# Output stores on ScalarE's queue, first weights kept by quarters, smaller feed-forward blocks and a changed plan in a recurrence-plus-feed-forward kernel

## Chip, cores and metric

One core of a Trainium2 chip. The metric is the device time of one execution in microseconds; a kernel's figure is the median of several executions. Executions of one kernel on one chip spread by about 1% here, some by up to 2%. An execution that lies more than 1.5% above the fastest of the same kernel is called slow, and the ratios leave it out. The granted clock is the share of its full clock that the profile shows for TensorE. Beside each kernel the kernel before was run in the same rounds, because chips differ: the medians of the kernel before lie between 197.7 and 199.8 us. Ratios in this document are the mean time of one kernel's fast runs over that of the other's of the same rounds, so they are not quite the ratio of the medians that are quoted. Brackets hold the 95% interval.

## What is computed

```python
def _attn_ref(r, k, v, w, u):                 # 4 batches, 8 heads, 768 steps, 48 wide
    state = np.zeros((B, H, D, D))
    for t in range(S):
        cur = einsum('bhd,bhe->bhde', u * k_t, v_t)
        y_t = einsum('bhd,bhde->bhe', r_t, state + cur)
        state = w_t[..., None] * state + einsum('bhd,bhe->bhde', k_t, v_t)

def _moe_ref(x, w_in, w_out):                 # x 3072x384, w_in 384x2048, w_out 2048x384
    h = x @ w_in
    g = np.maximum(0.01 * h, h)
    return g @ w_out
```

The recurrence's output, heads side by side, is x. Inputs and output are float32; the kernel multiplies in bfloat16.

## The kernel before

The 3072 tokens go in 24 chunks of 128. Each chunk has some twenty steps (log of the decays, cumulative sums, exponentials, the scaled r and k called `kr`, their transpose `rkT`, scores, mask, y, the new state, and y transposed into `xT`). Feed-forward blocks of 128 or 256 tokens follow: hidden matmuls into PSUM, activations on ScalarE, output matmuls, a copy, a store. (PSUM is where this kernel's matmuls write.)

Nothing is ordered by hand. Every step is entered with its engine, the time it is thought to take, the lag until others may use its result, and a rank; a small simulation (`Order`) sends out, one by one, whichever step can start first, and the kernel is emitted in that order. Each engine, and the one DMA queue of the sync engine, then works strictly in it.

```python
class Order:
    # cut: add, alias, ready
    def run(self, pools):
        # cut
        while any(todo.values()):
            best = None
            for eng, names in todo.items():
                loads = False
                for rank, seq, name in names:
                    # loads keep their order; stores and transposes may pass them
                    if eng == "DMA" and name[0] not in ("store", "rkT", "xT"):
                        if loads:
                            continue
                        loads = True
                    t = ready(name)
                    if t is None:
                        continue
                    t = max(t, free[eng])
                    key = (t, rank, seq)
                    if best is None or key < best[0]:
                        best = (key, eng, (rank, seq, name))
            # cut: send out best, advance free[eng], note the end

    w_in_b = const.tile([128, KT, FF], BF16, name="w_in_b")        # KT = 3, FF = 2048

    def cast_w_in(q):                                              # four quarters, on VectorE
        nc.vector.tensor_copy(out=w_in_b[:, :, q * FQ : (q + 1) * FQ], in_=stage["in", q][:])

    def a_rkT(i):                                                  # chunks 0 to 10
        if i < EARLY:                                              # EARLY = 5
            nc.scalar.copy(out=rkT[:], in_=att[i]["trp"][:])
        else:
            nc.vector.tensor_copy(out=rkT[:], in_=att[i]["trp"][:])

    def a_rkT_dma(i):                                              # chunks 11 to 23
        nc.sync.dma_start_transpose(out=rkT[:]..., in_=kr_b[i % NB3][:]...)

    sizes = [256, 256, 128, 128, 256, 128, 128, 256, 256, 256, 256, 256, 256, 256]

    def m_store(q, ts):
        nc.sync.dma_start(out=out[row : row + 128, :], in_=osbs.pop((q, ts))[:])

    Y_BY_DMA = range(15, NCH)
    WARM = 40.0          # filler matmuls on an idle tile keep TensorE's clock up until here
    RACT = 50            # rank of the feed-forward activations
    # cut
        add((x, n), "DMA", 1.06, load_in, n, x, lag=1.95, needs=past_user)        # w, r, k, v
            step("rkT", "DMA", 1.3, a_rkT_dma, "kr", *past(3, "mix"), lag=3.3)
            step("xT", "DMA", 0.6, a_ytr_dma, "ysb", "vsc", "t2", "st", lag=3.3)
            add(("store", q, ts), "DMA", 0.6, m_store, q, ts, lag=1.9, rank=-1, needs=[("copy", q, ts)])
```

Of the kernel before, what the change touches and what calls it, by code (L numbers as in the profile page):

```python
# [9 lines left out]
BF16 = mybir.dt.bfloat16  # L10
# [5 lines left out]
class Order:  # L16


    def __init__(self):
        self.steps = {}  # L20
        self.names = {}

    def add(self, name, eng, took, f, *args, lag=0.06, rank=0.0, needs=(), takes=()):
        self.steps[name] = (eng, took, f, args, lag, rank, list(needs), takes)
# [11 lines left out]
    def run(self, pools):  # L36
# [33 lines left out]
        while any(todo.values()):  # L70
            best = None
            for eng, names in todo.items():
                loads = False
                for rank, seq, name in names:
                    if eng == "DMA" and name[0] not in ("store", "rkT", "xT"):
                        if loads:
                            continue
                        loads = True
                    t = ready(name)
                    if t is None:  # L80
                        continue
                    t = max(t, free[eng])
                    key = (t, rank, seq)
                    if best is None or key < best[0]:
                        best = (key, eng, (rank, seq, name))
# [15 lines left out]
def kernel(  # L101
# [24 lines left out]
    NIN = 12  # L126
    EARLY = 5

# [3 lines left out]
    gpool = ctx.enter_context(tc.tile_pool(name="gpool", bufs=2))  # L132
    opool = ctx.enter_context(tc.tile_pool(name="opool", bufs=4))
    ps_cum = ctx.enter_context(tc.tile_pool(name="ps_cum", bufs=1, space=bass.MemoryType.PSUM))
# [13 lines left out]
    ukb = const.tile([128, DM], F32, name="ukb")  # L148
    w_in_b = const.tile([128, KT, FF], BF16, name="w_in_b")
    w_out_b = const.tile([128, NFT, NOUT], BF16, name="w_out_b")  # L150
# [37 lines left out]

    NQ = 4
    FQ = FF // NQ  # L190
# [17 lines left out]
    def cast_w_in(q):  # L208
        nc.vector.tensor_copy(out=w_in_b[:, :, q * FQ : (q + 1) * FQ], in_=stage["in", q][:])  # L209

# [176 lines left out]

    sizes = [256, 256, 128, 128, 256, 128, 128, 256, 256, 256, 256, 256, 256, 256]
    assert sum(sizes) == B * S
# [6 lines left out]
    def m_hid(q, j, nj):  # L396
        mb, t0 = sizes[q], starts[q]
        if j == 0:
            gts[q] = gpool.tile([128, NFT, mb], BF16, name="gt", tag="gt")
        hp = hps[q, j] = ps_mlp.tile([128, nj, mb], F32, name="hp", tag="mlp")  # L400
        for jj in range(nj):
            for t in range(KT):
                nc.tensor.matmul(  # L403
                    hp[:, jj, :], lhsT=w_in_b[:, t, (j + jj) * 128 : (j + jj + 1) * 128],
                    rhs=xT[:, t, t0 : t0 + mb], start=(t == 0), stop=(t == KT - 1),
                )
# [17 lines left out]
    def m_store(q, ts):  # L424
        row = starts[q] + ts * 128
        nc.sync.dma_start(out=out[row : row + 128, :], in_=osbs.pop((q, ts))[:])



    BY_DMA = range(11, NCH)  # L430
    Y_BY_DMA = range(15, NCH)
    WARM = 40.0
    RCAST = -1
    RACT = 50
    order = Order()
    add = order.add
    add("const", "POOL", 2.2, constants, rank=-1)
    users = []
    queue = [('in', 0), ('u', 0), ('in', 1), ('in', 2), ('w_in', 0), ('in', 3), ('w_in', 1), ('w_in', 2), ('w_in', 3), ('in', 4), ('w_out', 0), ('w_out', 1), ('w_out', 2), ('w_out', 3)] + [("in", i) for i in range(5, NCH)]
    for kind, n in queue:  # L440
# [4 lines left out]
        if kind == "in":  # L445
            for x in ("w", "r", "k", "v"):
                add((x, n), "DMA", 1.06, load_in, n, x, lag=1.95, needs=past_user)
            users.append(("done", n))
# [5 lines left out]
    for i in range(NCH):  # L454
# [17 lines left out]
        step("exn", "ACT", 0.52, a_exn, "neg", "exp")  # L472
        step("kr", "DVE", 1.05, a_kr, "exp", "exn", "k", "r", *past(3, "trans", "kv"))
        step("t1", "POOL", 1.0, a_t1, "r", ("u",), *past(2, "t2"))
        step("t2", "POOL", 1.15, a_t2, "t1", "k", *past(2, "diag"))
        step("vb", "ACT" if early else "POOL", 0.53, a_vb, "v", *past(3, "mix", "kv"))
        step("diag", "DVE", 0.55, a_diag, "t2", *past(3, "vsc"))
        step("vsc", "POOL", 0.86, a_vsc, "diag", "v", *past(3, "ysb"))
        if i in BY_DMA:
            step("rkT", "DMA", 1.3, a_rkT_dma, "kr", *past(3, "mix"), lag=3.3)  # L480
            order.alias(("trans", i), ("rkT", i))
        else:
            step("trans", "PE", 0.45, a_trans, "kr", *past(1, "rkT"), lag=0.3)
            step("rkT", "ACT" if early else "DVE", 1.0 if early else 0.69, a_rkT, "trans", *past(3, "mix"))
# [14 lines left out]
        if i in Y_BY_DMA:  # L499
            step("xT", "DMA", 0.6, a_ytr_dma, "ysb", "vsc", "t2", "st", lag=3.3)  # L500
            order.alias(("ytr", i), ("xT", i))
# [5 lines left out]
    for q, mb in enumerate(sizes):  # L507
# [8 lines left out]
        for ts in range(mb // L):  # L516
            for part in range(NQ):
# [5 lines left out]
            add(("copy", q, ts), "ACT", 0.48, m_copy, q, ts, rank=0, needs=[("out", q, ts, NQ - 1)]  # L523
                + [("store", *x) for x in tiles[-5:-4]])
            add(("store", q, ts), "DMA", 0.6, m_store, q, ts, lag=1.9, rank=-1, needs=[("copy", q, ts)])
    steps = order.run({"att": 3, "mlp": 3})
# [41 lines left out]
```

## Time and profile before

| | kernel before |
|---|---|
| median of 4 executions | 198.12 us (197.86 to 198.21) |
| profiled span, mean granted clock | 195.5 us, 1.000 |
| first output matmul starts | 43.82 us |
| 65th output matmul starts (4 of 24 output tiles done) | 59.80 us |
| last output copy starts | 192.21 us |
| TensorE time lost after 42 us | 10.9 us |
| of that, gaps over 0.25 us | 5.0 us |

The rows from "first output matmul" on are read from the starts of the single matmuls. They cut the run in two: a **start**, up to the 65th output matmul, and a **later part**, from there to the last copy (132.4 us here). "Lost" is the time to the next matmul's start beyond what the matmul itself takes.

The wait list of the sync engine's queue, kernel before. Its columns are: what waited, for whom, us in total, how many times, the longest. Its totals run over the whole span, so they include waits after the last load, which cost nothing; they are read for their order.

```profile
SPq L426 <- ACT osb L422: 24.4, 14, 7.4
SPq L299 <- DVE kr L256: 10.3, 10, 1.9
```

So two kinds of entries hold up the loads: stores (L426) that wait for their copy, and transposes (L299) that wait for `kr`.

The groups by shape of VectorE, kernel before (count | busy us, mean ns of one | idle before):

```profile
L209 DVE CAST w_in_b<-ws 128x1536 bf16<-128x1536 f32 x4 | 7.0, 1746 | 1.0 <-DMA ws<-in_moe_w_in_dram 1.0
```

And the chain that ended last, summed by engine, with the landing time of stores from the list of DMA issues:

```profile
PE 50%; DMA 20%; DVE 11%; SPq 9%; issue 5%; ACT 4%; DVEq 0%; ACTq 0%
...
out_dram<-osb SPq DMA_DIRECT2D x24, 192.0 KB, 2.2
```

### The profile page before, as it was taken

How to read it: one execution, taken by the hardware profiler on the slowest of the kernel's cores; microseconds unless marked ns; L12 is line 12 of the kernel's file. 1: busy time of each engine (PE TensorE's matmuls, PEld its weight loads, DVE VectorE, ACT ScalarE, POOL GpSimd, SP SyncE). 2: the span in 40 equal slices, each digit the busy share in tenths (PEclk: the TensorE clock that was granted, in tenths of full speed). 3: DMA queues.
4: the chain of work that ended last, by engine and by line, in shares of the span. 5: the costliest groups of instructions: out<-in, count | busy, mean ns of one | idle time of the engine just before them, and what ended most of it. 6: DMA issues, size and time to landing. Idle time of an engine off the chain costs nothing.

```text
span 195.5 us, 4886 instructions
## 1 busy us (share of the span) xinstructions
PE 182.2 (93%) x1921; PEld 130.0 (67%) x1926; DVE 115.7 (59%) x182; ACT 112.7 (58%) x219; POOL 111.3 (57%) x141
## 2 busy tenths in 40 slices
PE   7999697889999989999999997997999999999993
PEld 2455465765777758877777784774775876868661
DVE  2176997546479969996876776728457547300000
ACT  3565645872747476875587792482682762727310
POOL 3399554307457799999579688724757848100000
PEclk9999999999999999999999999999999999999999
DMA  6999899999499999999999998979989996221022
GB/s 126 203 188 249 225 376 149 358 330 142 129 198 210 195 203 215 187 169 190 156 230 207 184 161 167 213 149 168 213 181 190 217 166 126 64 62 40 3 80 80
DMA packets 124647, 34.70 MB, mean 177 GB/s; under 512 B 117840, under 2 KB 123088, under 8 KB 124624
## 3 DMA queue, kind: packets, MB, share of 16 engines
q1 hardware_dynamic: 124624, 34.38, 87.7%
q8 instruction: 15, 0.25, 0.5%
q14 instruction: 8, 0.07, 0.1%
HBM read 25.36 MB, written 4.72 MB: 154 GB/s over the span
## 4 chain that ended last, share of the span: by engine, by line
PE 50%; DMA 20%; DVE 11%; SPq 9%; issue 5%; ACT 4%; DVEq 0%; ACTq 0%
PE hp L403 21%; PE op L415 21%; DMA in<-in_w_dram 10%; DMA in<-in_k_dram 10%; SPq L184 7%; DVE mt L317 5%; DVE kr L256 2%; PE at L309 2%; DVE w_in_b L209 2%; ACT lw L224 1%; PE y L334 1%; PE cum L229 1%; PE trp L288 1%; PE ytr L375 1%; PE kv L347 1%
## 5 line engine op out<-in xcount | busy, mean ns | idle before, releaser
L403 PE MATMUL hp<-xT,w_in_b 128*128 128x256 bf16 (+1 forms) x672 | 71.5, 257 | 2.4 <-ACT gt L409 1.3
L415 PE MATMUL op<-w_out_b,gt 128*128 128x384 bf16 x384 | 68.8, 326 | 0.0
L409 ACT ACTIVATE gt<-hp 128x512 bf16<-128x512 f32 x96 | 55.8, 597 | 14.7 <-PE hp L403 12.6
L403 PEld LDWEIGHTS <-w_in_b 128*128 128x128 bf16 x672 | 56.2, 98 | 11.4 <-DVE w_in_b L209 2.0
L415 PEld LDWEIGHTS <-gt 128*128 128x128 bf16 x384 | 35.5, 98 | 20.6
L256 DVE TENSOR_TENSOR kr<-e,in 128x768 bf16<-128x768 f32 x24 | 28.1, 1169 | 19.5 <-DMA in<-in_k_dram 10.2
L317 DVE TENSOR_TENSOR mt<-at,tri 128x512 bf16<-128x512 f32 x48 | 31.0, 683 | 12.7 <-PE at L309 12.5
L264 POOL TENSOR_TENSOR t<-t,in 128x384 f32<-128x384 f32 x24 | 31.5, 1311 | 8.5 <-DMA in<-in_k_dram 7.4
L260 POOL TENSOR_TENSOR t<-in,ukb 128x384 f32<-128x384 f32 x24 | 24.0, 1000 | 16.6 <-DMA in<-in_r_dram 10.6
L365 POOL TENSOR_TENSOR st<-tt,e 48x192 bf16<-48x192 f32 x40 | 24.0, 600 | 16.6 <-DVE tt L355 15.1
L422 ACT COPY osb<-op 128x384 f32<-128x384 f32 x24 | 11.4, 477 | 30.5 <-PE op L415 30.2
L279 POOL TENSOR_TENSOR vsc<-in,diag 128x384 f32<-128x384 f32 x24 | 22.0, 916 | 8.6 <-DVE diag L275 5.8
L224 ACT ACTIVATE lw<-in 128x384 bf16<-128x384 f32 x24 | 12.5, 523 | 14.1 <-DMA in<-in_w_dram 14.1
L534 PE MATMUL scratch<-idle 128*128 128x512 bf16 x63 | 18.3, 415 | 1.4 <-DVE idle L166 1.3
L342 DVE TENSOR_TENSOR ysb<-y,vsc 128x384 bf16<-128x384 f32 x24 | 13.2, 552 | 5.4 <-PE y L334 4.1
L249 ACT ACTIVATE e<-cum 128x388 f32<-128x388 f32 x24 | 11.9, 496 | 7.4 <-PE cum L231 6.5
L275 DVE TENSOR_REDUCE diag<-t 128x8 f32<-128x384 f32 x24 | 13.1, 544 | 4.8 <-POOL t L264 4.6
L242 DVE SCALAR_TENSOR_TENSOR neg<-cum,lw 128x384 f32<-128x384 f32 x19 | 10.5, 553 | 9.0 <-ACT e L249 8.7
L271 POOL CAST vb<-in 128x384 bf16<-128x384 f32 x19 | 10.3, 542 | 4.2 <-DMA in<-in_v_dram 3.7
L252 ACT ACTIVATE e<-neg 128x384 f32<-128x384 f32 x19 | 9.9, 523 | 3.6 <-DVE neg L242 3.6
L534 PEld LDWEIGHTS <-idle 128*128 128x128 bf16 x68 | 6.5, 103 | 7.4 <-issue 1.9
L334 PE MATMUL y<-vb,mt 128*128 128x48 bf16 x192 | 9.2, 184 | 1.9 <-DVE mt L317 1.7
(43 smaller groups left out, 137.7 us busy)
## 6 DMA issues: line engine op xcount, KB each, us to landing
in<-in_w_dram SPq DMA_DIRECT2D x24, 192.0 KB, 4.3
in<-in_r_dram SPq DMA_DIRECT2D x24, 192.0 KB, 4.4
in<-in_k_dram SPq DMA_DIRECT2D x24, 192.0 KB, 4.3
in<-in_v_dram SPq DMA_DIRECT2D x24, 192.0 KB, 4.3
out_dram<-osb SPq DMA_DIRECT2D x24, 192.0 KB, 2.2
ws<-in_moe_w_in_dram SPq DMA_DIRECT2D x4, 768.0 KB, 6.7
ws<-in_moe_w_out_dram SPq DMA_DIRECT2D x4, 768.0 KB, 7.4
rkT<-kr SPq DMA_TRANSPOSE x13, 3.2
```

Source lines behind the costliest of these rows:

```text
L184: nc.sync.dma_start(out=ins[i][name], in_=src[b, :, c * L : (c + 1) * L, :].rearrange("h p d -> p h d"))
L224: nc.scalar.activation(out=lw_b[i % NB3][:, :, 0:D], in_=ins[i]["w"], func=AF.Ln)
L256: nc.vector.tensor_tensor(out=kr_b[i % NB3][:, :, 0:D], in0=e, in1=ins[i]["kr"], op=ALU.mult)
L260: nc.gpsimd.tensor_tensor(out=t1[:], in0=flat(ins[i]["r"]), in1=ukb[:], op=ALU.mult)
L264: nc.gpsimd.tensor_tensor(out=flat(t2[:]), in0=att[i]["t1"][:], in1=flat(ins[i]["k"]), op=ALU.mult)
L279: nc.gpsimd.tensor_tensor(out=vsc[:], in0=ins[i]["v"], in1=att[i]["diag"][:].unsqueeze(2).to_broadcast([128, H, D]), op=ALU.mult,)
L317: nc.vector.tensor_tensor(out=att[i]["mt"][:, x], in0=att[i]["ats"][x][:], in1=tri[:].unsqueeze(1).to_broadcast([128, NP, 128]), op=ALU.mult,)
L365: nc.gpsimd.tensor_tensor(out=sn[r0 : r0 + D, :, x * D : (x + 1) * D], in0=tt[r0 : r0 + D, :, x * D : (x + 1) * D], in1=el[r0 : r0 + D, :] ...
L403: nc.tensor.matmul(hp[:, jj, :], lhsT=w_in_b[:, t, (j + jj) * 128 : (j + jj + 1) * 128], rhs=xT[:, t, t0 : t0 + mb], start=(t == 0), stop= ...
L409: nc.scalar.activation(out=gts[q][:, j : j + nj, :], in_=hps.pop((q, j))[:], func=AF.Prelu, alpha=0.01)
L415: nc.tensor.matmul(ops[q, ts][:], lhsT=gts[q][:, j, ts * 128 : (ts + 1) * 128], rhs=w_out_b[:, j, :], start=(j == 0), stop=(j == NFT - 1),)
L534: nc.tensor.matmul(scratch[:], lhsT=idle[:, 0:128], rhs=idle[:], start=True, stop=True)
```

## The change

The intent: take stores that wait for a copy out of the queue that feeds the loads, and issue them on ScalarE right behind that copy; make each quarter of the first weights one run, so that its cast is quick; make most feed-forward blocks 128 tokens, so that a late chunk holds up less. With it come small numbers of the plan.

```diff
-    w_in_b = const.tile([128, KT, FF], BF16, name="w_in_b")
+    w_in_b = const.tile([128, NQ, KT, FF // NQ], BF16, name="w_in_b")
-        nc.vector.tensor_copy(out=w_in_b[:, :, q * FQ : (q + 1) * FQ], in_=stage["in", q][:])
+        nc.vector.tensor_copy(out=w_in_b[:, q], in_=stage["in", q][:])

-    sizes = [256, 256, 128, 128, 256, 128, 128, 256, 256, 256, 256, 256, 256, 256]
+    sizes = [256, 256, 128, 128, 128, 128, 128, 128, 128, 128, 128, 128, 128, 128, 128, 256, 128, 256, 256]

-        nc.sync.dma_start(out=out[row : row + 128, :], in_=osbs.pop((q, ts))[:])
+        nc.scalar.dma_start(out=out[row : row + 128, :], in_=osbs.pop((q, ts))[:])
# cut: the store becomes an "issue" step of ScalarE; output buffers 4 -> 6

# the plan's numbers
+                    if eng == "DMA" and waits and loads:      # waits: store, rkT or xT
+                        t += self.slack[name[0]]              # 1.2 us for rkT and xT
-            step("rkT", "DMA", 1.3, a_rkT_dma, "kr", *past(3, "mix"), lag=3.3)
+            step("rkT", "DMA", 1.6, a_rkT_dma, "kr", *past(3, "mix"), lag=2.2)
-            step("xT", "DMA", 0.6, a_ytr_dma, "ysb", "vsc", "t2", "st", lag=3.3)
+            step("xT", "DMA", 0.6, a_ytr_dma, "ysb", "vsc", "t2", "st", lag=2.4)
-    EARLY = 5
+    EARLY = 4
-    WARM = 40.0
+    WARM = 18.0
-    RACT = 50
+    RACT = 12
-    Y_BY_DMA = range(15, NCH)
+    Y_BY_DMA = range(14, NCH)
# cut: three planned times, 1.06 -> 1.07, 1.05 -> 1.08, 1.15 -> 1.2
```

The slack says: when a load could go now, plan a transpose 1.2 us after the time at which its data are thought to be ready.

More of the change, by code (lines that the diff above doesn't have):

```diff
@@ L21, in __init__ @@
         self.names = {}
+        self.slack = {}
     def add(self, name, eng, took, f, *args, lag=0.06, rank=0.0, needs=(), takes=()):
@@ L74, in run @@
                 for rank, seq, name in names:
-                    if eng == "DMA" and name[0] not in ("store", "rkT", "xT"):
+                    waits = name[0] in ("store", "rkT", "xT")
+                    if eng == "DMA" and not waits:
                         if loads:
@@ L126 @@
     NIN = 12
-    EARLY = 5
+    NOUTB = 6
+    NQ = 4
+    EARLY = 4
     const = ctx.enter_context(tc.tile_pool(name="const", bufs=1))
@@ L132 @@
     gpool = ctx.enter_context(tc.tile_pool(name="gpool", bufs=2))
-    opool = ctx.enter_context(tc.tile_pool(name="opool", bufs=4))
+    opool = ctx.enter_context(tc.tile_pool(name="opool", bufs=NOUTB))
     ps_cum = ctx.enter_context(tc.tile_pool(name="ps_cum", bufs=1, space=bass.MemoryType.PSUM))
@@ L187, in load_u @@
         nc.sync.dma_start(out=ukb[:], in_=u.rearrange("h d -> (h d)").partition_broadcast(128))
-    NQ = 4
     FQ = FF // NQ
@@ L401, in m_hid @@
         for jj in range(nj):
+            wq, f0 = divmod((j + jj) * 128, FQ)
             for t in range(KT):
                 nc.tensor.matmul(
-                    hp[:, jj, :], lhsT=w_in_b[:, t, (j + jj) * 128 : (j + jj + 1) * 128],
+                    hp[:, jj, :], lhsT=w_in_b[:, wq, t, f0 : f0 + 128],
                     rhs=xT[:, t, t0 : t0 + mb], start=(t == 0), stop=(t == KT - 1),
@@ L425, in m_store, with m_stored @@
         row = starts[q] + ts * 128
-        nc.sync.dma_start(out=out[row : row + 128, :], in_=osbs.pop((q, ts))[:])
+        nc.scalar.dma_start(out=out[row : row + 128, :], in_=osbs.pop((q, ts))[:])
+    def m_stored(q, ts):
+        pass
     BY_DMA = range(11, NCH)
-    Y_BY_DMA = range(15, NCH)
-    WARM = 40.0
+    Y_BY_DMA = range(14, NCH)
+    WARM = 18.0
     RCAST = -1
-    RACT = 50
+    SLACK = 1.2
+    RACT = 12
     order = Order()
+    order.slack = {"rkT": SLACK, "xT": SLACK, "store": 0.0}
     add = order.add
     add("const", "POOL", 2.2, constants, rank=-1)
+    users = []
+    users = []
     users = []
@@ L446 @@
             for x in ("w", "r", "k", "v"):
-                add((x, n), "DMA", 1.06, load_in, n, x, lag=1.95, needs=past_user)
+                add((x, n), "DMA", 1.07, load_in, n, x, lag=1.95, needs=past_user)
             users.append(("done", n))
@@ L472 @@
         step("exn", "ACT", 0.52, a_exn, "neg", "exp")
-        step("kr", "DVE", 1.05, a_kr, "exp", "exn", "k", "r", *past(3, "trans", "kv"))
+        step("kr", "DVE", 1.08, a_kr, "exp", "exn", "k", "r", *past(3, "trans", "kv"))
         step("t1", "POOL", 1.0, a_t1, "r", ("u",), *past(2, "t2"))
-        step("t2", "POOL", 1.15, a_t2, "t1", "k", *past(2, "diag"))
+        step("t2", "POOL", 1.2, a_t2, "t1", "k", *past(2, "diag"))
         step("vb", "ACT" if early else "POOL", 0.53, a_vb, "v", *past(3, "mix", "kv"))
@@ L523 @@
             add(("copy", q, ts), "ACT", 0.48, m_copy, q, ts, rank=0, needs=[("out", q, ts, NQ - 1)]
-                + [("store", *x) for x in tiles[-5:-4]])
-            add(("store", q, ts), "DMA", 0.6, m_store, q, ts, lag=1.9, rank=-1, needs=[("copy", q, ts)])
+                + [("store", *x) for x in tiles[-NOUTB - 1 : -NOUTB]])
+            add(("issue", q, ts), "ACT", 0.3, m_store, q, ts, rank=-1, needs=[("copy", q, ts)])
+            add(("store", q, ts), "DMA", 0.6, m_stored, q, ts, lag=1.9, rank=-1, needs=[("issue", q, ts)])
     steps = order.run({"att": 3, "mlp": 3})
```

## The prediction

> **What bounds the kernel now.** I read the page first (busy shares, slices), then the groups by shape, the chain that ended last, the sync engine's queue in order of time, and the starts of the single matmuls.
>
> ```profile
> PE 182.2 (93%) x1921; PEld 130.0 (67%) x1926; DVE 115.7 (59%) x182; ACT 112.7 (58%) x219; POOL 111.3 (57%) x141
> ...
> PE   7999697889999989999999997997999999999993
> ...
> PEclk9999999999999999999999999999999999999999
> DMA  6999899999499999999999998979989996221022
> ```
>
> TensorE is busy nearly throughout at full clock; the DMA engines are full until slice 34 (about 163 us) and then nearly idle. So there are two candidates, matmuls and input loads. "Busy" does not decide it, because matmuls overlap. The chain gives their real rate:
>
> ```profile
> 91.44 1.34 PE hp L403 x24
> ...
> 98.76 1.32 PE hp L403 x12
> ...
> 171.28 5.20 PE op L415 x32
> ```
>
> A 128-token hidden matmul takes 1.34/24 = 56 ns, a 256-token one 1.32/12 = 110 ns, an output one (384 columns) 5.20/32 = 163 ns. I gave every matmul in the trace its columns/2.4 ns + 2.5 ns and called the rest of the time to the next start "lost". Lost time: 7.7 us before 33 us (and 13.2 us of filler matmuls on the idle tile there), 2.2 us from 33 to 42, and from 42 us to the last matmul at 192.2 only 11.0 us out of 150. So from 42 us on the kernel is **matmul-bound with small leaks**; before that it is bound by what must happen ahead of the matmuls. Of the 11.0 us, 5.0 us are seven gaps over 0.25 us: at 68.4 (0.93), 75.4 (0.31), 119.6 (1.19), 134.2 (1.10), 135.3 (0.57), 149.6 (0.58) and 163.8 us (0.31). All but the one at 75.4 lead back to a late input load (the w load ahead of the log, or the k load ahead of kr): 4.7 us. The other 6 us are handovers of 0.1 to 0.2 us.
>
> The early stage is VectorE's. It is busy all of 20 to 30 us, and the first hidden matmuls wait for its weight casts:
>
> ```profile
> 25.72 1.74 DVE L209 CAST w_in_b<-ws 128x1536 bf16<-128x1536 f32 x1
> 27.38 1.28 DVE L317 TENSOR_TENSOR mt<-at,tri 128x512 bf16<-128x512 f32 x2
> 28.58 1.74 DVE L209 CAST w_in_b<-ws 128x1536 bf16<-128x1536 f32 x1
> 30.24 0.55 DVE L342 TENSOR_TENSOR ysb<-y,vsc 128x384 bf16<-128x384 f32 x1
> 30.70 0.55 DVE L355 TENSOR_TENSOR tt<-kv,st 128x384 f32<-128x384 f32 x1
> 31.17 1.74 DVE L209 CAST w_in_b<-ws 128x1536 bf16<-128x1536 f32 x1
> ```
>
> The late loads have a cause in the sync queue, which issues loads, transposes and stores in order:
>
> ```profile
> 43.98 2.37 SPq L184 DMA_DIRECT2D in<-in_w_dram  x1
> 49.97 1.27 SPq L426 DMA_DIRECT2D out_dram<-osb  x2
> 51.29 0.42 SPq L184 DMA_DIRECT2D in<-in_r_dram  x1
> ```
>
> From 46.4 to 50.0 us the queue stands at a store whose copy is not made yet, the next chunk's r, k and v behind it. The packets show the DMA engines at about 0.1 of their time from 48 to 51 us. Further waits of this kind before 163 us: 0.5, 0.9, 1.1, 1.1, 0.7, 0.2, 0.4 and 0.3 us; 8.7 us in all.
>
> **What the Trainium skill says.** (1) "VectorE: DVE Perf Modes", section "What auto-detection actually checks": a copy from fp32 runs at two elements a cycle only if the outermost dims of source and destination are both even or equal. A w_in quarter is now written as 3 rows of 512 out of 2048, a count of 3 against a source in one run; the new layout makes both one run of 1536, as w_out has it. The trace agrees: w_in casts take 1746 ns on the mean, w_out casts of as many elements 1116 ns (0.95 us for the shortest). (2) "TensorE: Matmul & The Clock Gate", section "Wait — 56ns, not 53.3ns?": columns over 2.4 GHz plus about 2.5 ns; the 56, 110 and 163 ns above agree, so two 128-token matmuls cost only about 2.5 ns more than one of 256. (3) "DMA: Bandwidth & Descriptors", section "Issuing engines are not separate DMA queues": a second issuing engine gives no bandwidth, only sequencer time. The trace shows what that time is: 0.33 to 0.56 us for a store's issue, beside the wait in front of it.
>
> **The change, part by part.**
> - *Weights by quarters.* Four casts go from 1.75 to about 0.95 us. All four stand in the VectorE-bound stretch; three lie on the chain between 22 and 33 us: 3 x 0.8 = 2.4 us. Not all of it reaches the end: the first output matmuls need w_out, which lands at VectorE only from 37 us on, and chunk 4's k load lands at 34.0 us in any case. I take **-2.0 us**.
> - *Stores off the sync queue.* 8.7 us of blocked waits and some 18 issues of about 0.45 us go from the queue that feeds the loads. The DMA engines have about 4 us of idle time to give back at 46 to 51 us and about 1.7 us at 131 to 133 us. Loads come up to 4 us sooner, which would close the 4.7 us of load gaps. But transposes still wait in that queue for VectorE (over 10 us in the wait list), so I take **-3.0 us**.
> - *The cost on ScalarE.* 24 issues of 0.33 to 0.56 us plus a wait for its own copy: some 0.5 us each, 12 us of occupation; ScalarE goes from 58% to about 65%. Per chunk it has 4 activations of 0.60, three of about 0.5, two copies of 0.48 and one issue: 5.4 us against 7 us of matmuls. It bites only where three PSUM buffers don't cover it: **+0.5 us**.
> - *Blocks of 128.* 14 of 19 blocks against 4 of 14: 912 hidden matmuls instead of 672, 240 x 2.5 ns = **+0.6 us**. The activation keeps its 128x512 shape and its count of 96. In return a block may start after one chunk instead of two, and a late chunk stalls less: **-0.8 us**.
> - *Small things.* 22 filler matmuls fewer, all before 42 us; chunk 4 moves its second cumulative sum and its transpose copy to VectorE, one more y transpose goes by DMA: 0.3 us of TensorE work less, **-0.3 us**. Output buffers go from 4 to 6: no wait on them shows now, so nothing.
>
> Sum: -2.0 -3.0 +0.5 +0.6 -0.8 -0.3 = -5.0 us. The tail (last copy, store, its landing: 3.3 us of the span) keeps its length. I hold back 0.4 us for what a new order always loses: **193.5 us**.
>
> **Rivals.**
> - *ScalarE inherits the blocking.* In the built program the DMAs share eight completion semaphores in rotation, so each waits for the DMA eight places before it, across queues. A store on ScalarE can thus stand still until a load or transpose issued by the sync engine lands, and the activations stand behind it in order. For it: loads take 4.3 us to land and issue at about 0.7 us each, so up to six are in flight. Against it: eight places is about 8 us of loads, and in the trace stores found that semaphore free. If it happens in most of the 18 stores before 163 us at 0.5 us or more, half reaching TensorE, it returns 4 us: 196 to 198 us.
> - *The loads are bound anyway.* With DMA engines at about 1.0 of their time from 54 to 163 us, clearing the queue moves waiting from the sequencer to the engines. Against: the idle at 46 to 51 us is real, and matmul work of 7 us a chunk is above the 6 to 6.5 us a chunk of DMA. Then only the start helps: 195 to 196 us.
> - *TensorE cools.* Without filler after 18 us the clock could drop before the first hidden matmuls; the page in (2), Part 1, gives an idle window of about 3.4 us as the condition. PEclk shows 9 in all slices now, and real matmuls fill about half of 18 to 33 us, so I give it little; it would cost about 1.5 us.
> - *All leaks close.* All 5 us of gaps and 3 us at the start go: about 190 us.
>
> **Range and chances.** The span cannot lose more than the 11 us leaked after 42 us and some 3 us at the start. Halfway between "only the start" and "all leaks close" lies 193. The 2% line is 194.1, close by, so: 190.3 to 197.2 for the range; faster 0.57, same 0.40, slower 0.03.
>
> **What would show it right or wrong.** Right: w_in casts near 1.0 us, and the last of them done by about 30.5 us; no store in the sync queue and no stretch from 46 to 51 us with empty DMA engines; the last v load landing near 157 us instead of 163; gaps over 0.25 us after 42 us summing to 2 us or less; activations still waiting on matmuls, not on stores. Wrong: ScalarE standing over 1 us at a store's semaphore, hidden matmuls waiting for activations by several us in the wait list, a 9 missing in PEclk, or the same load gaps with full DMA engines.

## The result

189.49 us (189.13 to 190.86, 4 executions): ratio 0.9579 [0.9531, 0.9628]. The same kernel on another chip gave 189.91 us, 0.9546 [0.9501, 0.9592] (the experiment r6 below). The gain is 8.6 us; 4.6 was predicted.

| | before | after | r6 |
|---|---|---|---|
| profiled span, us; clock | 195.5; 1.000 | 187.3; 0.988 | |
| first output matmul, us | 43.82 | 39.57 | 39.64 |
| 65th output matmul, us | 59.80 | 56.15 | 56.34 |
| last output copy, us | 192.21 | 184.08 | 183.98 |
| lost after 42 us | 10.9 | 6.4 | 6.1 |
| gaps over 0.25 us after 42 us | 5.0 | 1.35 | 1.2 |
| last load issued, us | 158.5 | 153.9 | 153.7 |

The start gives 3.65 us, the later part 4.5 us (132.4 to 127.9), of which 3.65 us are closed gaps. That is nearly the prediction's rival "all leaks close".

The page of the kernel after: busy shares, slices, chain by engine, and the stores' row of DMA issues (last column: us from issue to landing).

```profile
PE 177.5 (95%) x2140; PEld 133.0 (71%) x2140; DVE 114.3 (61%) x184; ACT 110.4 (59%) x216; POOL 113.6 (61%) x142
...
PEclk9999978999999999999999999999999999999999
DMA  6999899899999999999999999699999999612012
...
PE 74%; SPq 11%; DMA 9%; ACT 2%; issue 2%; DVE 1%; POOL 0%; ACTq 0%; DVEq 0%
...
out_dram<-osb ACTq DMA_DIRECT2D x24, 192.0 KB, 3.5
```

TensorE's share of the chain went from 50% to 74%, that of DMA from 20% to 9%. The 4 in the eleventh DMA slice is gone. A 7 and an 8 appeared in PEclk. A store takes 3.5 us to land instead of 2.2.

The timeline of ScalarE around the second store, kernel after:

```profile
46.34 0.48 ACT L428 COPY osb<-op 128x384 f32<-128x384 f32 x1 [0.22 <-PE op L421]
46.85 0.37 ACTq L432 DMA_DIRECT2D out_dram<-osb  x1
47.32 0.49 ACT L254 ACTIVATE e<-cum 128x388 f32<-128x388 f32 x1 [0.51 <-POOL t L265]
```

The issue starts 0.03 us after the copy's end and takes 0.37 us (0.34 on the mean). At all 24 stores the semaphore waits were found free. In the sync queue's timeline of the kernel after, loads follow each other where the queue stood at a store before:

```profile
46.28 0.92 SPq L190 DMA_DIRECT2D in<-in_r_dram  x1
47.25 0.70 SPq L190 DMA_DIRECT2D in<-in_k_dram  x1
```

The casts, in VectorE's groups by shape and timeline, kernel after:

```profile
L214 DVE CAST w_in_b<-ws 128x1536 bf16<-128x1536 f32 x4 | 3.9, 969 | 1.2 <-DMA ws<-in_moe_w_in_dram 1.0
```
```profile
25.32 0.96 DVE L214 CAST w_in_b<-ws 128x1536 bf16<-128x1536 f32 x1
27.61 0.96 DVE L214 CAST w_in_b<-ws 128x1536 bf16<-128x1536 f32 x1
30.68 0.95 DVE L214 CAST w_in_b<-ws 128x1536 bf16<-128x1536 f32 x1
```

1746 ns became 969, but the last cast ends only 1.3 us sooner (31.6 against 32.9 us). The second and third casts start within 0.03 us of the landing of their loads (25.29 and 27.59 us). The last one's load lands at 29.70 us; it stands on VectorE behind `ysb`, which waited 1.17 us for a matmul, and that matmul came after twelve hidden matmuls at a lowered clock (shown last in this section).

Part of the start has nothing to do with casts. Timeline of all engines, kernel before, then after, around 38 us:

```profile
38.23 1.01 ACT L293 COPY rkT<-trp 128x1024 bf16<-128x1024 bf16 x1 [0.67 <-PE trp L288]
39.14 1.09 ACT L409 ACTIVATE gt<-hp 128x512 bf16<-128x512 f32 x2
...
39.80 0.82 PE L403 MATMUL hp<-xT,w_in_b 128*128 128x256 bf16 x6 [1.00 <-ACT gt L409]
```
```profile
38.03 1.91 ACT L415 ACTIVATE gt<-hp 128x512 bf16<-128x512 f32 x3 [0.60 <-PE hp L409]
38.09 0.68 DVE L300 COPY rkT<-trp 128x1024 bf16<-128x1024 bf16 x1
...
39.57 2.12 PE L421 MATMUL op<-w_out_b,gt 128*128 128x384 bf16 x12
```

Before, chunk 4's transpose copy stands on ScalarE for 1.01 us ahead of two activations, and the hidden matmuls that need their PSUM buffers wait 1.00 us. After (EARLY 4) that copy is VectorE's, the activations run beside it, and the first output matmul starts at 39.57 us.

Last, the clock. Stretches of the kernel after (us, PE busy and count, PEclk, DMA share, GB/s), then the first slow hidden matmuls in the timelines of after and before:

```profile
22.00:25.00 3.00, 2.05 (x34) 1.00 0.98 335
25.00:29.00 4.00, 3.06 (x22) 0.62 1.06 365
```
```profile
26.33 2.74 PE L409 MATMUL hp<-xT,w_in_b 128*128 128x256 bf16 x12 [0.34 <-DVE w_in_b L214]
```
```profile
27.62 1.47 PE L403 MATMUL hp<-xT,w_in_b 128*128 128x256 bf16 x12
```

The rival "TensorE cools" came true: twelve matmuls took 2.74 us instead of 1.47. It was also one of the signs that the prediction listed as wrong (a 9 missing in PEclk).

### The profile page after: what moved, and what is told of

It reads as the page before. It is cut to its first block, busy times and chain, and to the rows that moved or that the text cites. A ratio compares the mean times of both kernels' runs of the same rounds, so it can differ in the third digit from the quotient of the medians.

```text
span 187.3 us, 5286 instructions
## 1 busy us (share of the span) xinstructions
PE 177.5 (95%) x2140; PEld 133.0 (71%) x2140; DVE 114.3 (61%) x184; ACT 110.4 (59%) x216; POOL 113.6 (61%) x142
## 4 chain that ended last, share of the span: by engine, by line
PE 74%; SPq 11%; DMA 9%; ACT 2%; issue 2%; DVE 1%; POOL 0%; ACTq 0%; DVEq 0%
PE hp L409 30%; PE op L421 30%; SPq L190 9%; PE at L314 3%; DMA in<-in_r_dram 3%; DMA in<-in_w_dram 3%; DMA ws<-in_moe_w_in_dram 3%; PE cum L234 2%; PE y L339 2%; PE trp L293 2%; PE y L333 1%; PE kv L352 1%; DVE w_in_b L214 1%; PE ytr L380 1%; PE cum L236 1%
## 5 line engine op out<-in xcount | busy, mean ns | idle before, releaser
L409 PE MATMUL hp<-xT,w_in_b 128*128 128x128 bf16 (+1 forms) x912 | 72.5, 235 | 0.7 <-DVE w_in_b L214 0.7
L421 PE MATMUL op<-w_out_b,gt 128*128 128x384 bf16 x384 | 69.7, 326 | 0.0
L409 PEld LDWEIGHTS <-w_in_b 128*128 128x128 bf16 x912 | 62.0, 98 | 6.8 <-DVE w_in_b L214 1.1
L415 ACT ACTIVATE gt<-hp 128x512 bf16<-128x512 f32 x96 | 55.4, 597 | 14.4 <-PE hp L409 11.7
L370 POOL TENSOR_TENSOR st<-tt,e 48x192 bf16<-48x192 f32 x40 | 25.9, 648 | 22.5 <-DVE tt L360 19.2
L265 POOL TENSOR_TENSOR t<-in,ukb 128x384 f32<-128x384 f32 x24 | 26.2, 1090 | 13.2 <-DMA in<-in_r_dram 6.7
L269 POOL TENSOR_TENSOR t<-t,in 128x384 f32<-128x384 f32 x24 | 27.8, 1159 | 5.9 <-DMA in<-in_k_dram 4.8
L229 ACT ACTIVATE lw<-in 128x384 bf16<-128x384 f32 x24 | 12.5, 521 | 13.7 <-DMA in<-in_w_dram 13.2
L347 DVE TENSOR_TENSOR ysb<-y,vsc 128x384 bf16<-128x384 f32 x24 | 13.3, 554 | 10.5 <-PE y L339 8.8
L247 DVE SCALAR_TENSOR_TENSOR neg<-cum,lw 128x384 f32<-128x384 f32 x20 | 11.0, 552 | 13.9 <-ACT e L254 13.9
L254 ACT ACTIVATE e<-cum 128x388 f32<-128x388 f32 x24 | 11.9, 495 | 10.5 <-PE cum L236 3.8
L548 PE MATMUL scratch<-idle 128*128 128x512 bf16 x46 | 13.3, 429 | 1.3 <-DVE idle L172 1.3
L276 POOL CAST vb<-in 128x384 bf16<-128x384 f32 x20 | 12.6, 629 | 2.8 <-DMA in<-in_v_dram 2.5
L257 ACT ACTIVATE e<-neg 128x384 f32<-128x384 f32 x20 | 10.5, 524 | 5.6 <-DVE neg L247 5.0
L314 PE MATMUL at<-rkT 48*128 48x128 bf16 x192 | 9.5, 219 | 1.9 <-ACT rkT L298 1.9
L234 PE MATMUL cum<-lw,tri 128*128 128x384 bf16 x24 | 8.0, 335 | 1.9 <-ACT lw L229 1.9
```

Of the source, the lines that this page charges most:

```text
L265: nc.gpsimd.tensor_tensor(out=t1[:], in0=flat(ins[i]["r"]), in1=ukb[:], op=ALU.mult)
L269: nc.gpsimd.tensor_tensor(out=flat(t2[:]), in0=att[i]["t1"][:], in1=flat(ins[i]["k"]), op=ALU.mult)
L314: nc.tensor.matmul(ats[x][:, p, :], lhsT=rkT[r0 : r0 + D, 0, p, :], rhs=rkT[r0 : r0 + D, 1, p, :], start=True, stop=True,)
L347: nc.vector.tensor_tensor(out=ysb[:], in0=att[i]["y"][:], in1=flat(att[i]["vsc"][:]), op=ALU.add)
L370: nc.gpsimd.tensor_tensor(out=sn[r0 : r0 + D, :, x * D : (x + 1) * D], in0=tt[r0 : r0 + D, :, x * D : (x + 1) * D], in1=el[r0 : r0 + D, :] ...
L409: nc.tensor.matmul(hp[:, jj, :], lhsT=w_in_b[:, wq, t, f0 : f0 + 128], rhs=xT[:, t, t0 : t0 + mb], start=(t == 0), stop=(t == KT - 1),)
```

## The experiments

The theory on going in: the three named parts do it, and stores on ScalarE give most. The first rival: the plan's numbers, which the prediction hardly costed, do a good part. So each part was run **alone** on the kernel before and **undone** alone in the kernel after. All runs gave correct results. Figures in profiles are from one execution each. The kernel after itself ran in other rounds than the undone versions, so "undone" effects compare two ratios to the kernel before, not runs side by side; below about half a per cent they are not resolved.

One caution on the profiles. In e5, e6 and p1 TensorE gets the kernel after's matmuls in the same order up to 50 us at least, yet their first output matmul starts at 41.1 to 42.0 us instead of 39.6. In e5 and p1 the clock was also down for longer (e5: 0.54 from 26 to 30 us and 0.61 from 30 to 34; kernel after: 0.58 and 1.00). So starts of single profiles differ by up to 2.4 us with no edit in them, and they cannot place an effect of that size.

### Each part alone

**e1: only the layout by quarters.** Same order of instructions as before.

```diff
-    w_in_b = const.tile([128, KT, FF], BF16, name="w_in_b")
+    w_in_b = const.tile([128, 4, KT, FF // 4], BF16, name="w_in_b")
-        nc.vector.tensor_copy(out=w_in_b[:, :, q * FQ : (q + 1) * FQ], in_=stage["in", q][:])
+        nc.vector.tensor_copy(out=w_in_b[:, q], in_=stage["in", q][:])
```

> The kernel before with only the new layout of the input weights (quarters one after another); the order of all instructions is the same as before. Theory A (the start is bound by the four casts, and what it gains goes through to the end): casts near 0.97 us instead of 1.75, 2 to 3.5 us faster, 194.6 to 196.1 us. Theory B (my prediction's caution: the output weights and chunk 4's loads hold the start anyway): under 1 us faster, 197.1 us or more.

Measured: 197.08 us, 0.9941 [0.9894, 0.9988], about -1.2 us. First output matmul 43.11 us, 0.7 earlier. VectorE's groups by shape in e1:

```profile
L209 DVE CAST w_in_b<-ws 128x1536 bf16<-128x1536 f32 x4 | 4.4, 1106 | 2.0 <-DMA ws<-in_moe_w_in_dram 2.0
```

2.6 us of cast time are gone, and the casts' own wait for their loads doubled from 1.0 to 2.0 us: the layout works, and the next limit, the weight load, takes back a part.

**e2: only the stores on ScalarE**, with six output buffers.

```diff
-        nc.sync.dma_start(out=out[row : row + 128, :], in_=osbs.pop((q, ts))[:])
+        nc.scalar.dma_start(out=out[row : row + 128, :], in_=osbs.pop((q, ts))[:])
-            add(("store", q, ts), "DMA", 0.6, m_store, q, ts, lag=1.9, rank=-1, needs=[("copy", q, ts)])
+            add(("issue", q, ts), "ACT", 0.3, m_store, q, ts, rank=-1, needs=[("copy", q, ts)])
+            add(("store", q, ts), "DMA", 0.6, m_stored, q, ts, lag=1.9, rank=-1, needs=[("issue", q, ts)])
```

> The kernel before with only the stores issued from ScalarE's queue (and six output buffers); blocks, layout and the other numbers of the planner as before. Theory A (stores at the head of the sync queue held up the loads): the DMA idle time at 46 to 51 us is gone, lost time after 42 us falls from 11.0 to about 7, 3 to 4 us faster, 194 to 195 us. Theory B (the smaller blocks closed the gaps, not the queue): under 1 us faster, gaps over 0.25 us still 4 us or more.

Measured: 197.21 us, 0.9961 [0.9921, 1.0000]: -0.8 us, an interval that touches zero. Gaps after 42 us did not shrink (6.1 us against 5.0). These are theory B's numbers, but not for its reason: e3 shows that the blocks did not close the gaps. The sync queue's wait list and the DMA slices of e2:

```profile
SPq L299 <- DVE kr L256: 14.5, 9, 4.9
```
```profile
DMA  6999999999998999639999998999999985121022
```

The store wait is gone and the eleventh slice is full, but the transposes now wait 14.5 us for `kr` where they waited 10.3, and the idle of the DMA engines turned up in the 17th and 18th slices (78 to 88 us). The sync queue's timeline there, e2:

```profile
78.96 0.84 SPq L184 DMA_DIRECT2D in<-in_k_dram  x1
84.76 1.42 SPq L299 DMA_TRANSPOSE rkT<-kr  x1
86.22 0.57 SPq L184 DMA_DIRECT2D in<-in_v_dram  x1
```

Between 79.80 and 84.76 us the queue stands at a transpose, with v behind it; its `kr` ends at 84.7 us. The wait was not removed; **it moved to the next in-order entry that was not ready.** The kernel after has the same order in that place, but its `kr` ends at 80.8 us, and the queue stands for 1.1 us:

```profile
78.81 0.93 SPq L190 DMA_DIRECT2D in<-in_k_dram  x1
80.88 1.96 SPq L304 DMA_TRANSPOSE rkT<-kr  x1
82.88 0.57 SPq L190 DMA_DIRECT2D in<-in_v_dram  x1
```

**e3: only the block sizes.** (The old `sizes` line for the new one.)

```diff
-    sizes = [256, 256, 128, 128, 256, 128, 128, 256, 256, 256, 256, 256, 256, 256]
+    sizes = [256, 256, 128, 128, 128, 128, 128, 128, 128, 128, 128, 128, 128, 128, 128, 256, 128, 256, 256]
```

> The kernel before with only the new block sizes (14 of 19 blocks of 128 tokens). Theory A (queue): the finer blocks alone bring little, within 1 us of 198.1, as stores still block the queue, even earlier and oftener. Theory B (finer blocks let TensorE go on when a chunk is late): 2 to 4 us faster, 194 to 196 us, with fewer gaps over 0.25 us.

Measured: 199.21 us, 1.0067 [1.0013, 1.0121]: +1.3 us. Gaps after 42 us 6.0 us. Alone the small blocks lose.

**e9: only the plan's numbers**, all of them, nothing else.

```diff
+    order.slack = {"rkT": 1.2, "xT": 1.2, "store": 0.0}
-    EARLY = 5
+    EARLY = 4
-    WARM = 40.0
+    WARM = 18.0
-    RACT = 50
+    RACT = 12
# and Y_BY_DMA, the transposes' planned times and lags, three planned times, as in the change
```

> The kernel before with only the planner's numbers of the change: assumed times and lags of transposes, a slack of 1.2 us that lets loads pass a transpose not yet ready, early chunks 4 instead of 5, filler up to 18 instead of 40 us, one more y transpose by DMA, the rank of the activation. Stores, layout and blocks as before. Theory P (the planner's numbers are the main part, as layout, stores and blocks alone gave -0.6, -0.4 and +0.7%): 3 to 6 us faster, 192 to 195 us. Theory S (only the parts together work): within 1.5 us of before.

Measured: 197.22 us, 0.9895 [0.9864, 0.9925]: the largest of the four alone, about -2.1 us, between the two theories. In its profile the start is ahead (first output matmul 41.56 us, 65th 58.51), by less than starts differ without an edit; gaps after 42 us are 7.1 us. The sync queue's wait list of e9 begins with the stores as before, and the wait for `kr` has left its top nine lines:

```profile
SPq L430 <- ACT osb L426: 24.5, 15, 7.4
```

Four of those nine lines put 13.7 us of the transposes' waits down to matmuls; measured as standing before their issue they are 1.9 us (table further down), while their issues grew from 15.6 to 20.5 us. That is e2's mirror image: there stores were cleared and transposes stood; here transposes mostly go without standing and stores stand. The four alone multiply to 0.9941 x 0.9961 x 1.0067 x 0.9895 = 0.986. Together they give 0.955 to 0.958. **The parts need each other.**

### Each part undone

**e7: the kernel after with all of the plan's numbers as before.**

```diff
-    order.slack = {"rkT": SLACK, "xT": SLACK, "store": 0.0}
+    order.slack = {"rkT": 0.0, "xT": 0.0, "store": 0.0}
-    EARLY = 4
+    EARLY = 5
# and WARM, RACT, Y_BY_DMA, planned times and lags back
```

> The changed kernel with only those planner's numbers put back; stores on ScalarE, layout and blocks as changed. Theory P: most of the gain is gone, 195 to 198 us. Theory S: it keeps half or more, 190 to 193.5 us.

Measured: 200.09 us, 1.0006 [0.9967, 1.0045]. All of the gain is gone: **the three named parts together, on the old plan, are worth nothing.** Lost time after 42 us is 14.0 us, gaps 8.3 us.

**e4: the old weight layout.** Same order as the kernel after.

```diff
-    w_in_b = const.tile([128, NQ, KT, FF // NQ], BF16, name="w_in_b")
+    w_in_b = const.tile([128, KT, FF], BF16, name="w_in_b")
```

> The changed kernel with only the old layout of the input weights put back; the order of all other instructions is the same. If the layout's gain is passed on to the end in full: 2 to 3.5 us slower than the changed kernel, 191.5 to 193 us, casts back at 1.75 us. If the better-fed later part absorbs it: under 1 us slower, 190.5 us or less.

Measured: 190.89 us, 0.9638 [0.9597, 0.9679]: the layout is worth 0.6 to 0.9%, as in e1. All six executions of e4 have a granted clock of 0.980 to 0.982, those of the kernel after mostly 0.988 to 0.991, so a part of it may be the clock.

**e5: stores back on the sync queue.**

```diff
-        nc.scalar.dma_start(out=out[row : row + 128, :], in_=osbs.pop((q, ts))[:])
+        nc.sync.dma_start(out=out[row : row + 128, :], in_=osbs.pop((q, ts))[:])
```

> The changed kernel with only the stores put back on the sync queue (six buffers kept). If stores at the queue's head cost what I predicted: 3 us slower than the changed kernel or more, 192.5 us or above, and loads late after 46 us again. If it is off the path: within 1 us, 188.5 to 190.5 us.

Measured: 194.66 us, 0.9745 [0.9721, 0.9770]: with the new plan the stores' place is worth 1.7 to 2.0%, some 3.3 to 4 us, against 0.4% alone. Gaps after 42 us 4.0 us.

**e6: old block sizes.** The `sizes` line of before.

```diff
-    sizes = [256, 256, 128, 128, 128, 128, 128, 128, 128, 128, 128, 128, 128, 128, 128, 256, 128, 256, 256]
+    sizes = [256, 256, 128, 128, 256, 128, 128, 256, 256, 256, 256, 256, 256, 256]
```

> The changed kernel with only the old block sizes. If finer blocks matter once the rest is changed: 2 us slower or more, 191.5 us or above. If they don't, as alone (+0.7%): within 1 us of the changed kernel.

Measured: 191.65 us, 0.9604 [0.9562, 0.9647]. The kernel after lies at 0.9546 to 0.9579, with overlapping intervals: 0.3 to 0.6%, not resolved.

**p1: old plan for the transposes only** (no slack; planned times and lags as before).

```diff
-    order.slack = {"rkT": SLACK, "xT": SLACK, "store": 0.0}
+    order.slack = {"rkT": 0.0, "xT": 0.0, "store": 0.0}
-            step("rkT", "DMA", 1.6, a_rkT_dma, "kr", *past(3, "mix"), lag=2.2)
+            step("rkT", "DMA", 1.3, a_rkT_dma, "kr", *past(3, "mix"), lag=3.3)
-            step("xT", "DMA", 0.6, a_ytr_dma, "ysb", "vsc", "t2", "st", lag=2.4)
+            step("xT", "DMA", 0.6, a_ytr_dma, "ysb", "vsc", "t2", "st", lag=3.3)
```

> The changed kernel (0.958 of before) with only the planner's numbers for DMA transposes put back: no slack, rkT time 1.3 and lag 3.3, xT lag 3.3. Theory T (the slack and lags, which decide how many loads stand ahead of a transpose in the sync queue, are what made the planner's part matter): ratio to before 0.985 or above. Otherwise 0.955 to 0.970.

Measured: 194.24 us, 0.9808 [0.9762, 0.9853]: the transposes' plan is worth 2.3 to 2.6%, the largest single item, though less than theory T asked for (0.985 or above). In p1 transposes stand up to two loads sooner in the queue. The sync queue's timelines of p1, then of the kernel after, at the same transpose:

```profile
124.68 1.23 SPq L304 DMA_TRANSPOSE rkT<-kr  x1
125.96 0.57 SPq L190 DMA_DIRECT2D in<-in_r_dram  x1
```
```profile
123.17 0.57 SPq L190 DMA_DIRECT2D in<-in_r_dram  x1
124.00 1.99 SPq L304 DMA_TRANSPOSE rkT<-kr  x1
```

The r load behind the transpose goes out at 125.96 us, in the kernel after ahead of it at 123.17 us. How much of that is the order cannot be read here: the two queues have the same order up to about 78 us, and p1's profile was 2.8 us late by its 65th output matmul (58.96 us). Its later part is 2.3 us longer (130.2 us).

**p2: EARLY back to 5.**

```diff
-    EARLY = 4
+    EARLY = 5
```

> The changed kernel with only EARLY back at 5, so that chunk 4's second cumulative sum runs on TensorE into one of the three feed-forward PSUM buffers and its transpose copy on ScalarE. Theory E (this freed the start: the changed kernel is 3.5 us ahead at 42 us, of which layout alone gives 0.7): ratio 0.970 or above, lost plus filler before 42 us up by 2 us or more. Otherwise 0.955 to 0.965.

Measured: 192.22 us, 0.9703 [0.9660, 0.9745]. With EARLY 5 chunk 4's second cumulative sum goes from VectorE to TensorE, its transpose copy from VectorE and its cast of v from GpSimd to ScalarE; that costs 1.2 to 1.6%. The profile cannot show where: its first output matmul starts at 42.41 us instead of 39.57, but with the long drop of the clock (0.54 and 0.61 from 26 to 34 us) that e5 shows too, which has EARLY 4 and starts at 41.77 us.

**p3: activation rank back to 50.**

```diff
-    RACT = 12
+    RACT = 50
```

> The changed kernel with only the rank of the activation back at 50 (it then stands behind the attention steps of every chunk on ScalarE, not only of chunks up to 12). Theory R (from about 100 us on, activations come late and hold the hidden matmuls, or attention comes late): ratio 0.970 or above, lost time after 100 us up by 2 us or more. Otherwise 0.955 to 0.965.

Measured: 190.27 us, 0.9596 [0.9557, 0.9634]: not resolved.

**p4: filler matmuls up to 40 us again.** The order of the other instructions stays.

```diff
-    WARM = 18.0
+    WARM = 40.0
```

> The changed kernel with filler matmuls put back up to 40 us; all real instructions in the same order. Theory C (the clock dip at 25 to 29 us, twelve hidden matmuls in 2.74 instead of 1.47 us, reaches the end): 1 to 1.3 us faster than the changed kernel, ratio 0.951 to 0.955, clock 1.000. If the DMA-bound arrival of the output weights hides it: the same within 0.3%.

Measured: 190.78 us, 0.9621 [0.9571, 0.9671] (fast runs). The dip of the clock is gone in the profile (9 in every slice of PEclk), and the time is no better; the intervals overlap.

### Do stores and transposes together make the later part?

The theory had become: loads stand behind whatever is not ready at the head of the sync queue, and clearing one kind moves the wait to the other.

**r1: the kernel before with stores on ScalarE and the transposes' plan, nothing else.** **r5: r1 with EARLY 4 as well.**

```diff
 # r1: e2's edit, and
+    order.slack = {"rkT": 1.2, "xT": 1.2, "store": 0.0}
+            step("rkT", "DMA", 1.6, a_rkT_dma, "kr", *past(3, "mix"), lag=2.2)
+            step("xT", "DMA", 0.6, a_ytr_dma, "ysb", "vsc", "t2", "st", lag=2.4)
 # r5: that, and
+    EARLY = 4
```

> The kernel before with exactly two things: stores on ScalarE's queue, and the slack and lags that let loads pass a transpose that is not ready. Layout, blocks, EARLY, filler, rank as before. Theory H (the loads wait at the sync queue's head behind stores and behind transposes; clearing one only moves the wait to the other, clearing both is what pays): 3.5 to 5 us faster than before, ratio 0.975 to 0.982, gaps over 0.25 us after 42 us at 2.5 us or less. Rival I (the planner's numbers act as a whole, through the match of plan and chip): ratio 0.988 or above.

> As r1, and EARLY 4 instead of 5. Theory H with the start's part in chunk 4's path: a further 1.5 to 2.5 us, ratio 0.965 to 0.972, first output matmul near 41.5 us instead of 43.8. If EARLY only acts with the new layout: within 0.5% of r1.

Measured, same chip and rounds: r1 196.14 us, 0.9837 [0.9782, 0.9892]; r5 194.43 us, 0.9759 [0.9713, 0.9806]. In r1 the later part fell from 132.4 to 128.9 us, which neither e2 (131.8) nor e9 (133.0) had done, and gaps after 42 us to 3.3 us. But its start was 2 us late in that profile (65th output matmul at 61.78 us), its ratio lies between what the theory and the rival asked for, and it is not resolved from the product of e2 and e9, 0.986. So the later part speaks for the theory, the total time alone does not resolve it. EARLY gave a further 0.8%, some 1.5 us, the low end of what was expected; the first output matmul moved from 45.15 to 42.33 us, of which some 1.3 us is r1's own lateness (the kernel before, in the same order up to there, has 43.82). The DMA slices of r1 have none under 6 before the loads end, where e2 had its 3.

**r2: stores on the sync queue, but planned 3 us after their copy.** If the wait at the head were the whole cost of a store there, this should be nearly as good as ScalarE.

```diff
-        nc.scalar.dma_start(out=out[row : row + 128, :], in_=osbs.pop((q, ts))[:])
+        nc.sync.dma_start(out=out[row : row + 128, :], in_=osbs.pop((q, ts))[:])
-    order.slack = {"rkT": SLACK, "xT": SLACK, "store": 0.0}
+    order.slack = {"rkT": SLACK, "xT": SLACK, "store": 3.0}
```

> The changed kernel with the stores on the sync queue, each put 3 us later in that queue by the planner, so that its copy should be done when its turn comes. With the stores back at their old places it was 0.9745. Theory H (the wait at the queue's head is the cost): 0.958 to 0.966. Theory Q (what the sync engine's issue time of about 0.45 us a store costs is the point, so that another engine has to issue): 0.970 or above.

Measured: 194.04 us, 0.9736 [0.9672, 0.9800]; no better than e5's 0.9745. From the trace, the sync engine's time between 44 and 161 us divides like this (us):

| | at a store, before its issue | stores' issue | at an `rkT` transpose, before its issue | last load issued |
|---|---|---|---|---|
| before | 10.0 | 7.1 | 9.4 | 158.5 |
| e2 | - | - | 13.9 | 156.7 |
| e9 | 9.6 | 7.6 | 1.9 | 162.9 |
| e5 | 10.8 | 8.8 | 1.6 | 160.5 |
| r2 | 1.7 | 15.5 | 3.0 | 158.8 |
| after | - | - | 8.9 | 153.9 |
| r6 | - | - | 6.0 | 153.7 |

r2 did take the wait away (10.8 to 1.7 us), and most of it came back as issue: 15.5 us instead of 8.8; four of the 17 stores take 1.5 to 2.2 us each to issue. **So the theory, that the wait at the head is the cost, is refuted as the whole story.** It may be that a store in this queue costs its place among the loads as well. The table shows the same elasticity elsewhere: in the kernel after the 72 loads take 68.1 us to issue where 71 took 55.6 before, so of 10.5 us less waiting (24.8 to 14.3, all kinds) only 4.6 us come out as an earlier last load. And it warns against reading one column: the kernel after still waits 8.9 us for transposes, and e9, with hardly any, issued its last load latest.

**r3: slack 2.4 instead of 1.2.**

```diff
-    SLACK = 1.2
+    SLACK = 2.4
```

> The changed kernel with a slack of 2.4 instead of 1.2 us. If loads still lose time behind transposes: 0.5 to 1 us faster, ratio 0.951 to 0.955. If transposes then come late and hold the scores: slower, 0.962 or above.

Measured: 194.52 us, 0.9661 [0.9568, 0.9755] (the two fast runs of five, 191.45 and 193.22 us). No gain from more slack is shown; the interval takes in the kernel after's ratio, so a loss is not shown either. The slower the run, the lower its clock (0.991 at 191.45 us, 0.965 at 197.64 us).

**r6: the kernel after, again.**

> The changed kernel, unchanged: 0.953 to 0.963 of before, with a clock dip in the profile somewhere between 18 and 36 us.

Measured: 189.91 us (188.76 to 191.55), 0.9546 [0.9501, 0.9592], given with the result above.

**r4: seven more fillers, at half density, from 18 to 32 us**, to hold the clock at less cost.

```diff
-    WARM = 18.0
+    WARM = 32.0
-                for _ in range(int((start - at) / 0.22)):
+                for _ in range(int((start - at) / (0.22 if start < 18.0 else 0.44))):
```

> The changed kernel with seven more filler matmuls, spread from 18 to 32 us at half the old density. If the dip costs time and filler standing ahead of real matmuls was what ate the gain at full density: 0.5 to 1.5 us faster than the changed kernel, clock 1.000. If the dip is hidden behind the arrival of weights and chunks: the same within 0.3%.

Measured in r6's rounds: 190.61 us, 0.9543 [0.9500, 0.9585], clock 0.991. The dip stayed (0.57 from 22 to 26 us, as in r6), the time is r6's. No version better than the kernel after was found.

### All together

| part | alone, against before | undone, against the kernel after |
|---|---|---|
| all of the plan's numbers | -1.05% | +4.3 to +4.6 points |
| transposes' slack, times and lags | not run alone | +2.3 to +2.6 |
| stores on ScalarE | -0.4% | +1.7 to +2.0 |
| EARLY 4 | not run alone; -0.8% from r1 to r5 | +1.2 to +1.6 |
| weights by quarters | -0.6% | +0.6 to +0.9 |
| less filler | not run alone | +0.4 to +0.8, intervals overlap |
| blocks of 128 | +0.7% | not resolved |
| activation rank 12 | not run alone | not resolved |

The second column is each undone version's ratio less 0.9579 and less 0.9546. It sums, without the first row, to some 6 to 8 points, well above the total gain of 4.2 to 4.5%: the mark of parts that each need the others.

## Why the prediction was wrong

The direction was right, 193.5 us with 190.3 at the low end was too cautious: 189.49 and 189.91 us.

- **The step that failed is "Small things ... -0.3 us".** It took the plan's numbers for what they move in TensorE work (a cumulative sum, a transpose). It did not name the slack and the lags at all. The runs put -1.05% (about -2.1 us) on them alone (e9), +4.3 to +4.6 points on undoing them (e7), 2.3 to 2.6% on the transposes' plan alone (p1) and 1.2 to 1.6% on EARLY (p2). In an order-driven kernel they are the order in which the one sync queue serves loads and transposes and in which the engines serve the steps. The sum itself failed with it: it adds parts as if each kept its worth alone, and the four alone give 0.986, all together 0.955 to 0.958.
- **"Stores off the sync queue, -3.0 us"**: as an addition to the old kernel it was -0.8 us at best (e2), because transposes took over the wait. The prediction saw that ("transposes still wait in that queue") and had no number for it, nor did it see that the slack in the same diff was the answer to it. Undone from the new kernel the part is worth 3.3 to 4 us (e5). The size was right only in company.
- **Weights by quarters, -2.0 us**: mechanism right (969 ns), size too high: -1.2 us alone, 1.2 to 1.8 us undone. The casts' wait for their loads doubled in e1; the prediction named later loads as limits, not these.
- **ScalarE, +0.5 us, and the rival that it inherits the blocking**: the rival is refuted, and of the +0.5 us no sign is seen. The issue costs 0.34 us, the semaphore waits were found free, activations wait 11.7 us for matmuls in the wait list (12.6 before).
- **Blocks, +0.6 and -0.8 us**: alone +1.3 us (e3), in the new kernel at best a small gain (e6). Not a cause of the result.
- **"TensorE cools"**: happened (0.62 from 25 to 29 us) and was given little chance. Filling up to 40 us removes the dip and gains nothing (p4), but the filler itself takes TensorE time, so what the dip alone costs was not isolated. Single executions do not settle it: in e6 those with a clock of 0.973 and 0.982 took 192.8 and 193.2 us, the others (0.990 and 0.991) 190.5 to 192.2 us; in p1 one with 0.982 took 194.24 us and two with 1.000 took 193.2 and 194.25 us.
- **"The loads are bound anyway"**: it seems true in part. Of 10.5 us less waiting in the queue 4.6 us reached the last load, while the issues of loads and transposes grew longer.
- **"All leaks close, about 190 us"** is the rival that came closest, in its number: it had the parts that the prediction named close the leaks, and without the plan's numbers they close none (e7: gaps 8.3 us). Its ceiling of "some 3 us at the start" was low: the start gave 3.65 us.
- Of the signs listed as right, most appeared: casts near 1.0 us, no store in the sync queue, gaps under 2 us (1.35), activations waiting on matmuls. The last cast was late (31.6 us against 30.5) and the last loads went out earlier than thought.

What stays open is the exact split of the later part. That stores and transposes hold up loads in turn is shown by e2, e9 and the timelines. That the named parts and the plan's numbers together give more than alone is shown by e7, e9 and the undone versions; for stores and the transposes' plan by themselves r1's total does not show it. A rival was not tested: every edit of the plan also shuffles other entries, and an order may simply fit by luck. Only one other slack was tried (r3), and slow runs blurred it. Why a store that waits for nothing is still dear in the sync queue (r2) is narrowed to its issue and its place among the loads, not settled between the two; r2's plan also moves other entries.

## What to carry to other kernels

When an order is made by a plan, cost the plan's constants in a diff first, as moves of instructions on each in-order queue; those that look like calibration can carry more than the named parts. Taking an entry off the head of an in-order queue pays only as far as the next entry is ready: look for what would stand there next. Test each part alone and undone: alone the stores looked worth 0.4%, undone 2%, and neither number by itself tells what they are.

## What the Trainium skill lacked or had wrong

- "DMA: Bandwidth & Descriptors", section "Issuing engines are not separate DMA queues", says that issuing from several engines saves only the sequencer's time, usually small beside the DMA. Here it was not small: 24 stores put back on the sync engine cost 1.7 to 2.0% (e5), and the same when they mostly no longer stood waiting (r2: 15.5 us of issue instead of 8.8).
- "TensorE: Matmul & The Clock Gate", Part 1, gives an idle window of about 3.4 us in its table as what lowers the clock; the same part also says that frequent small idles can make it swing, but not how much idleness does. Here it fell to 0.62 between 25 and 29 us although TensorE's longest pause from 18 to 30 us was 0.97 us; it was busy 58% of the time from 18 to 26 us (4.61 of 8 us). The kernel before was busy for 6.21 of these 8 us and kept its clock.
- No page of the skill that we found treats the planned order of waiting entries on an in-order DMA queue as a cost of its own; here it was worth 2.3 to 2.6% (p1).
